# Attention with two gated layers on one core: later rounds for weight pieces and softmax reciprocals, marked copies, and two fill units in the scores' banks

## The chip, the cores and the metric

The kernel runs on one core of one Trainium2 chip, as a single launch. The metric is the time of one execution in device microseconds; smaller is better. The time before is a median of three runs. All times below are microseconds (us) unless marked ns.

## The reference

Three layers follow each other. Shapes: 2 batches, 12 heads, 448 positions, 64 columns a head; so the model width is 768, and the hidden width 1024.

```python
# 1. attention with a soft cap
scores = cap * tanh((q @ k.T) / sqrt(64) / cap)
attn   = exp(scores - max(scores))
attn   = attn / (sum(attn) + 1e-9)
x      = attn @ v                       # heads side by side: 2 x 448 x 768
# 2. gated layer with spatial mixing
h      = gelu_tanh(x @ w_in)            # 768 -> 1024
u, v   = halves of h                    # 512 each
v      = layernorm(v) * g_ln
v      = einsum('ts,bsd->btd', w_sg, v) + b_sg
x      = x + (u * v) @ w_out            # 512 -> 768
# 3. gated convolution
h      = relu(x @ w2_in)
c      = conv of 3 taps along positions
out    = (h * sigmoid(c)) @ w2_out
```

## The kernel before

**Attention.** Two heads make a pair; there are 12 pairs, N = 0 to 11. A pair is worked in two halves, so the loop `for R in range(2 * NN + LAGS[1])` has 26 rounds. In a round TensorE makes the scores of one half (`sc`, 4 PSUM banks, one buffer), and then, two rounds late, the products with the values and the sums of an earlier half (`pv`, 3 banks). ScalarE does two passes over each half: Tanh out of the bank (L387) and Exp in place (L388), so that the next scores can start once Tanh has read the banks. At the end of a pair ScalarE copies the products and the sums out of PSUM into `E` (L504); the next products wait for that copy.

**The softmax division.** For pairs 0 to 10 it is done off the path: GpSimd's queue moves the sums by DMA into a compact tile `ss` (L506), VectorE adds a guard and takes the reciprocal (L519, L520), DMAs spread it over the partitions as `rb` (L523, L529), and VectorE multiplies (L536); the result is split in a high and a low part, `X` (L105, L106). For the last pair, 11, there is no time for that: `norm_pe` copies the sums (L548), VectorE adds the guard and takes a reciprocal of 224 columns (L550, L551), and TensorE spreads it by multiplying with a selection matrix `sel` (L555).

**Pieces.** The weights come as 64-bit words and are converted on the chip. `w_in` comes in 12 pieces of 128x512, one per entry of `WIN`, which names the round of its load. A piece has three steps: s1 takes the top bits into a head tile `hd` (L149 on ScalarE, L151 on VectorE for the early ones), s2 joins them with the low bits (L154) and makes the high part (L160), s3 makes the low part (L163). There is one head tile, so a piece's s1 must wait for the s2 of the piece before it.

**What sets the order.** `later(k, fn)` puts a step k ticks ahead; a round has two ticks, one before and one after its value products. A scheduler then orders the instructions of each engine from this program. `pin(lasta)` and `pin(lastv)` keep a step behind the last marked instruction of ScalarE or VectorE. `ordered` keeps the attention's matmuls in the order written; matmuls of the later stages are not held by it. TensorE, ScalarE and VectorE each run their list in order, so that a waiting instruction holds all behind it.

**Fill units.** The first layer's units (`u_unit`, 18 matmuls each of 128x448) need the first weights and batch 0 only. Three of them are taken into attention as fill: `FILL` gives the round and which of the six steps. Each is summed in the single bank `mo` of pool `psm` and then goes through `gelu`: ScalarE L221, VectorE L224, ScalarE L225, VectorE L228. The next unit in that bank waits for L228. The fourth unit, here called unit 3 (L109 to L111), also uses the bank. After it come the units of the second half of `w_in` (`v_unit`, L724 to L726), and from there on matmuls alone.

**Names.** PE is TensorE, ACT ScalarE, DVE VectorE, POOL GpSimd, SP the queue of most loads. The lines that count: L149/L151, L154, L160, L163 (piece), L387, L388 (scores), L504 (copy of values), L519, L520 (sums), L536 (division), L548 to L559 (last pair), L221 to L228 (gelu).

Of the kernel before, what the change touches and what calls it, by code (L numbers as in the profile page):

```python
# [9 lines left out]
F32 = mybir.dt.float32  # L10
F32R = mybir.dt.float32r
U32 = mybir.dt.uint32
# [3 lines left out]
AF = mybir.ActivationFunctionType  # L16
# [3 lines left out]
P = 128  # L20
B, H, S, D = 2, 12, 448, 64
NPAIR = H // 2
DM, DF, DH = 768, 1024, 512
NK = DM // P
# [3 lines left out]
HS = S // 2  # L28
# [5 lines left out]

NFAST = 1

FILL = {14: (0, 0, 2), 18: (0, 2, 4), 22: (0, 4, 6), 23: (1, 0, 6), 25: (2, 0, 6)}

TAKEN = 3

# [1 line left out]

IDLE = 4

WIN = (3, 5, 8, 10, 12, 14, 15, 17, 18, 20, 21, 22)
WOS = (0, 1, 4, 7, 7, 10, 11, 15)
W2I = (12, 12, 13, 13, 15, 17, 22, 24, 26, 30, 30, 33)
W2O = (0, 0, 1, 3, 4, 6, 7, 8, 8, 10, 10, 11, 11, 11, 11, 12, 13, 14, 15, 17, 18, 18, 19, 19)
# [3 lines left out]
def stages(  # L52
# [17 lines left out]
    nc = tc.nc  # L70
    V, A, T, G = nc.vector, nc.scalar, nc.tensor, nc.gpsimd

    now = [0]
    lasta, lastv, lastr, lasts = [None], [None], [None], [None]

    def pin(last):
        return tc.issue_after(last[0].ins) if last[0] is not None else ExitStack()
# [11 lines left out]
    def later(k, fn):  # L89
        due.setdefault(now[0] + k, []).append(fn)  # L90
# [7 lines left out]
    def f(ap):  # L98
        return ap.bitcast(F32)
# [19 lines left out]
    psm = ctx.enter_context(tc.tile_pool(name="psm", bufs=1, space=PSUM))  # L119
# [12 lines left out]
    heads = []  # L132
# [35 lines left out]
    def decode(hi, lo, src, pool, bufs, wait=(1, 2, 3), hi_eng="a", cols=512, low_eng="v", top_eng="a"):  # L168

        if heads:  # L170
            return decode_half(hi, lo, src, pool, bufs, wait, hi_eng, top_eng)
        n = src.shape[1]
        r = pool.tile([P, cols, 2], U32, tag="f64", name="f64", bufs=bufs)[:, :n]
        sync(r, src)
        h, l = r[:, :, 1], r[:, :, 0]

        def s1():
            with pin(lasta), pin(lastv):
                A.activation(f(h), f(h), AF.Copy, scale=2.0**-112)  # L179
                if low_eng == "a":  # L180

                    A.activation(l, l, AF.Copy, scale=0.93 * 2.0**-29)  # L182
                else:
                    V.tensor_scalar(
                        out=l, in0=l, scalar1=29, scalar2=None, op0=ALU.logical_shift_right
                    )

        def s2():
            V.scalar_tensor_tensor(  # L189
                out=l, in0=h, scalar=3, in1=l, op0=ALU.logical_shift_left, op1=ALU.bitwise_or  # L190
            )
            V.scalar_tensor_tensor(  # L192
                out=l, in0=h, scalar=0x80000000, in1=l, op0=ALU.bitwise_and, op1=ALU.bitwise_or
            )
            if hi_eng == "a":
                A.activation(hi, f(l), AF.Copy)
            else:
                V.tensor_copy(hi, f(l))

        def s3():  # L200
            V.tensor_tensor(out=lo, in0=f(l), in1=f(hi), op=ALU.subtract)

        for k, fn in zip(wait, (s1, s2, s3)):
            later(k, fn)

    def wdec(dst, src, k, c0, c1, pool, bufs, **kw):
        c = slice(c0 % dst.shape[3], c0 % dst.shape[3] + c1 - c0)
        decode(dst[:, 0, k, c], dst[:, 1, k, c], src[k * P : (k + 1) * P, c0:c1], pool, bufs, **kw)

    def wi_piece(src, h, k):  # L210
        return WI[h], src, k, h * DH, (h + 1) * DH
# [34 lines left out]
    def constants(pool):  # L246
        V.tensor_scalar(
            out=capc, in0=capt, scalar1=CAP_MAX, scalar2=-CAP_MAX, op0=ALU.min, op1=ALU.max
        )
        V.reciprocal(out=rcap, in_=capc if bounded else capt)  # L250
        V.tensor_scalar(
            out=qscale, in0=rcap, scalar1=1.0 / math.sqrt(D), scalar2=None, op0=ALU.mult
        )

        V.tensor_scalar(out=ncap, in0=capc, scalar1=-1.0, scalar2=None, op0=ALU.mult)
        V.tensor_tensor(out=ncap, in0=ncap, in1=capc, op=ALU.min)
        A.activation(guard, ncap, AF.Exp)
        V.tensor_scalar(out=guard, in0=guard, scalar1=1e-9, scalar2=None, op0=ALU.mult)
        heads[:] = [pool.tile([P, 512], U32, name=f"hd{i}") for i in range(1)]
        for t in heads:  # L260
            G.memset(f(t), 0.0)
        eye = pool.tile([P, P], F32, name="eye")
        make_identity(nc, eye)
        G.memset(nhalf, -0.5)
        return eye

    def columns(pool):
        sync(gbc, g_ln.partition_broadcast(P))
        decode(cw[:, 0], cw[:, 1], conv_w, pool, 4 if bounded else 3)

    def attention(att, psa):
# [218 lines left out]
        def norm(N, both):  # L490
            b, p = divmod(N, NPAIR)
            if N >= B * NPAIR - NFAST:
                return norm_pe(N, both)

            j = N % 2
            last = N == B * NPAIR - NFAST - 1
            m = 1 if last else 2
            if j == 0:
                pairs[:] = (
                    att.tile([P, 2 * (S + HS)], F32, tag="E", name="E", bufs=3),  # L500
                    att.tile([P, 14], F32, tag="ss", name="ss", bufs=2)[:, : 7 * m],
                )
            e, ss = pairs
            A.activation(e[:, j * (S + HS) : (j + 1) * (S + HS)], both, AF.Copy)  # L504
            u = j * (2 * S + HS)
            G.dma_start(ss[j * P // m : (j + 1) * P // m], e[::32, u : u + HS])  # L506
            if j == 0 and not last:
                return

            rb = att.tile([P, 2, S], F32, tag="rb", name="rb", bufs=2)  # L510
            eb = e[:, HS : HS + m * S].rearrange("p (j c) -> p j c", j=m)
            rb = rb[:, :m]

            ds = []


            def s1():
                with pin(lastv):
                    V.tensor_scalar(out=ss, in0=ss, scalar1=guard, scalar2=None, op0=ALU.add)  # L519
                V.reciprocal(out=ss, in_=ss)  # L520
                ds.append(dr.tile([m, 2, 2, HS], F32, tag=f"d{m}", name="d"))
                d = ds[0]
                G.dma_start(d.rearrange("j h f (p c) -> (j h f p) c", c=7 * m), ss)  # L523

            def s1b():
                (d,) = ds
                for h in range(2):
                    for i in range(m):
                        G.dma_start(  # L529
                            rb[h * D : (h + 1) * D, i].rearrange("p (f c) -> p f c", f=2),  # L530
                            d[i, h].partition_broadcast(D),
                        )

            def s2():
                with pin(lastv):
                    V.tensor_tensor(out=eb, in0=eb, in1=rb, op=ALU.mult)  # L536
                with pin(lasta):
                    lastv[0] = split(eb, X[:, 0, p - j : p + 1, b], X[:, 1, p - j : p + 1, b], "a")

            later(4, s1)  # L540
            later(5, s1b)
            later(13, s2)

        def norm_pe(N, both):

# [17 lines left out]
        fill = {}  # L563
        done = 0
        for R in range(2 * NN + LAGS[1]):
            N, half = divmod(R, 2)
            if R == 1:
                columns(att)
            if R == 4:
                load_vlast(3, NN)  # L570
            for j, at in enumerate(WIN):
                if at == R:
                    top_eng = "v" if R < 11 else "a"
                    wdec(*wi_piece(w_in, j // NK, j % NK), att, 4, hi_eng="v", wait=(3, 4, 5), top_eng=top_eng)
            if R < 2 * NN:
                if half == 0 and N + 2 < NN:
                    load(N + 2)
                if half == 0 and N + 1 < NN:
                    load_v(N + 1)
                if R == 1:  # L580

                    start_values(0)
                    scores(N, half, {2: lambda: value(0, 0), 3: lambda: value(0, 1)})
                    values(0, 0, True)
                    done += 1
                else:
                    scores(N, half)
                if half == 0 and N + 1 < NN:
                    prep_q(N + 1)
                    prep_k(N + 1)  # L590
            if R in FILL:

                i, k0, k1 = FILL[R]
                if k0 == 0:
                    fill[i] = psm.tile([P, 512], F32, tag="mo", name="mo")[:, :S]
                for k in range(k0, k1):
                    mmw(fill[i], 0, i, k, ordered)
                if k1 == NK:
                    u_done(0, i, fill[i])
            tick()  # L600
            if R - done >= LAGS[R >= LAGS[2]]:
                values(*divmod(done, 2))
                done += 1
            tick()
# [414 lines left out]
```

## Time and profile before

| | us |
|---|---|
| median of 3 runs | 335.48 (333.1 to 338.03) |
| the profiled execution | 337.11 |
| its span, first to last instruction | 335.3 |
| TensorE busy | 318.5 (95%) |
| VectorE busy | 238.3 (71%) |
| ScalarE busy | 223.2 (67%) |
| GpSimd busy | 37.6 (11%) |
| mean granted TensorE clock | 0.985 |

The kernel is a relay: attention up to about 121 us, where four engines and the DMA queues work side by side, and then dense matrix products to the end. A share of the whole span says little here; the views have to be read by stage. In a timeline row the columns are start, length, engine, line and operation, out<-in, shape, count; "idle" in brackets is the time the engine stood still just before and what ended it. In a windows row they are the stretch, its length, busy time (and instructions) of PE, PE's weight load, DVE, ACT, POOL, then the granted TensorE clock (1.00 is 2.4 GHz, 0.50 is 1.2 GHz), the DMA share and GB/s.

### The profile page before, as it was taken

What the parts mean: (1) busy time and instruction counts of PE and PEld (TensorE: products, weight loads), DVE (VectorE), ACT (ScalarE), POOL (GpSimd) and SP (SyncE); (2) the same over time, 40 slices, a digit from 0 to 9 for tenths busy, and PEclk for the clock granted to TensorE, in tenths of its full rate; (3) what the DMA queues carried; (4) which work ended last, traced back from release to release, by engine and by line L of the source; (5) the groups of instructions that cost most, each with busy time, mean ns of one, the idle gap of its engine ahead of it and who ended that gap; (6) DMA issues with size and microseconds to landing.
All of it is one profiled execution on the core that took longest, in us unless ns stands there. A gap on an engine that the chain in (4) does not pass through costs nothing.

```text
span 335.3 us, 6265 instructions
## 1 busy us (share of the span) xinstructions
PE 318.5 (95%) x2380; PEld 262.8 (78%) x2380; DVE 238.3 (71%) x471; ACT 223.2 (67%) x357; POOL 37.6 (11%) x74
## 2 busy tenths in 40 slices
PE   7979999999788999999999999999999999999992
PEld 6445666656556778988899999999999999999991
DVE  4556586585965589996998789996975999980000
ACT  2887999999896257675765565555855988873010
POOL 4000130440304320221111000000000000000000
PEclk9978999999999999999999999999999999999998
DMA  5586595778422134212323490002392123012211
GB/s 141 150 193 187 154 259 171 199 216 189 133 75 76 38 123 108 69 38 78 121 71 125 124 343 20 0 2 63 71 334 100 31 65 94 0 59 112 82 55 35
DMA packets 22062, 37.73 MB, mean 113 GB/s; under 512 B 7320, under 2 KB 14376, under 8 KB 22024
## 3 DMA queue, kind: packets, MB, share of 16 engines
q1 hardware_dynamic: 20152, 34.41, 34.3%
q0 software_dynamic: 1632, 2.61, 3.1%
q8 instruction: 20, 0.33, 0.4%
q10 hardware_dynamic: 240, 0.23, 0.3%
q14 instruction: 18, 0.15, 0.2%
HBM read 34.40 MB, written 2.79 MB: 111 GB/s over the span
## 4 chain that ended last, share of the span: by engine, by line
PE 79%; ACT 10%; DMA 4%; SPq 2%; issue 2%; DVE 1%; ACTq 0%; DVEq 0%
PE mo L109 18%; PE mo L110 18%; PE mo L111 18%; PE pv L373 8%; PE sc L373 6%; ACT raw L387 4%; PE mo L724 3%; PE mo L726 3%; PE mo L725 3%; SPq L83 2%; ACT raw L388 2%; PE mo L373 2%; DMA qr<-in_qT_dram 1%; ACT hd L149 1%; DMA f<-in_conv_w_dram 1%
## 5 line engine op out<-in xcount | busy, mean ns | idle before, releaser
L109 PE MATMUL mo<-X,WI 128*128 128x448 f32 x126 | 46.0, 367 | 0.3 <-DVE u L228 0.3
L110 PE MATMUL mo<-X,WI 128*128 128x448 f32 x126 | 46.0, 366 | 0.0
L111 PE MATMUL mo<-X,WI 128*128 128x448 f32 x126 | 45.9, 365 | 0.0
L373 PE MATMUL pv<-raw,V 128*32 128x224 f32 x576 | 34.6, 370 | 3.5 <-ACT E L504 3.3
L388 ACT ACTIVATE raw<-raw 128x1792 f32<-128x1792 f32 (+3 forms) x26 | 36.7, 1413 | 0.8
L387 ACT ACTIVATE raw<-sc 128x1792 f32<-128x1792 f32 (+1 forms) x22 | 32.4, 1472 | 5.0 <-PE sc L373 4.9
L110 PE MATMUL mo<-HG,W 128*128 128x448 f32 x96 | 34.8, 365 | 0.0
L111 PE MATMUL mo<-HG,W 128*128 128x448 f32 x96 | 34.7, 365 | 0.0
L109 PE MATMUL mo<-HG,W 128*128 128x448 f32 x96 | 34.1, 365 | 0.0
L373 PE MATMUL sc<-Q,K 64*128 64x448 f32 x216 | 29.9, 399 | 3.8 <-ACT raw L387 3.3
L373 PEld LDWEIGHTS pv<-raw,V 128*32 128x32 f32 x576 | 19.1, 112 | 16.6 <-ACT E L504 6.0
L373 PEld LDWEIGHTS sc<-Q,K 64*128 64x128 f32 x216 | 19.1, 192 | 14.7 <-ACT raw L387 8.1
L179 ACT ACTIVATE f<-f 128x256 f32<-128x256 f32 (+2 forms) x44 | 22.8, 518 | 10.2 <-DMA f<-in_w_out_dram 6.2
L189 DVE SCALAR_TENSOR_TENSOR f<-f 128x256 uint32<-128x256 uint32 (+2 forms) x44 | 22.3, 515 | 8.2 <-ACT f L182 8.0
L109 PEld LDWEIGHTS mo<-X,WI 128*128 128x128 f32 x126 | 23.6, 188 | 2.8 <-DVE u L228 0.8
L110 PEld LDWEIGHTS mo<-X,WI 128*128 128x128 f32 x126 | 23.7, 188 | 2.0
L111 PEld LDWEIGHTS mo<-X,WI 128*128 128x128 f32 x126 | 23.6, 188 | 2.0
L904 ACT ACTIVATE o<-mo 128x448 f32<-128x448 f32 x12 | 6.3, 542 | 24.7 <-PE mo L111 20.8
L182 ACT ACTIVATE f<-f 128x256 uint32<-128x256 uint32 (+2 forms) x44 | 22.7, 515 | 0.0
L192 DVE SCALAR_TENSOR_TENSOR f<-f 128x256 uint32<-128x256 uint32 (+2 forms) x44 | 22.4, 515 | 0.1
L110 PEld LDWEIGHTS mo<-HG,W 128*128 128x128 f32 x96 | 18.0, 188 | 1.4
L109 PEld LDWEIGHTS mo<-HG,W 128*128 128x128 f32 x96 | 18.0, 188 | 1.4
(148 smaller groups left out, 685.8 us busy)
## 6 DMA issues: line engine op xcount, KB each, us to landing
f<-in_w_in_dram SPq DMA_DIRECT2D x12, 512.0 KB, 4.4
f<-in_w_out_dram SPq DMA_DIRECT2D x24, 256.0 KB, 4.5
f<-in_w_in_dram SPq DMA_DIRECT2D x12, 511.8 KB, 5.1
f<-in_w_out_dram SPq DMA_DIRECT2D x8, 384.0 KB, 3.1
qr<-in_qT_dram SPq DMA_DIRECT2D x24, 112.0 KB, 3.7
out_dram<-o SPq DMA_DIRECT2D x12, 224.0 KB, 1.9
rb<-d POOLq DMA_DIRECT2D x22, 112.0 KB, 4.0
V<-in_vL_dram SPq DMA_DIRECT2D x12, 192.0 KB, 3.3
```

The costliest lines, as they stand in the source:

```text
L109: matmul(ps, lhsT=whi, rhs=xhi, start=start, stop=False)
L110: matmul(ps, lhsT=whi, rhs=xlo, start=False, stop=False)
L111: matmul(ps, lhsT=wlo, rhs=xhi, start=False, stop=stop)
L179: A.activation(f(h), f(h), AF.Copy, scale=2.0**-112)
L182: A.activation(l, l, AF.Copy, scale=0.93 * 2.0**-29)
L189: V.scalar_tensor_tensor(out=l, in0=h, scalar=3, in1=l, op0=ALU.logical_shift_left, op1=ALU.bitwise_or)
L192: V.scalar_tensor_tensor(out=l, in0=h, scalar=0x80000000, in1=l, op0=ALU.bitwise_and, op1=ALU.bitwise_or)
L373: lastm[0] = T.matmul(*args, **kw)
L387: A.activation(x, ps, AF.Tanh, **sc)
L388: lasta[0] = A.activation(x, x, AF.Exp, scale=creg)
L724: T.matmul(ps, lhsT=xs(0, k), rhs=WI[1][:, 0, k], start=k == 0, stop=False)
L725: T.matmul(ps, lhsT=xs(0, k), rhs=WI[1][:, 1, k], start=False, stop=False)
```

## The change

It has seven parts: (1) the copy of values into `E` now marks `lasta`, so that a piece's s1 that comes later in the program cannot be put ahead of it; (2) two head tiles in place of one; (3) the identity matrix is made only in the fallback program that does not run here; (4) for pairs below 8, s1 and s1b of the sums come two ticks later and s2 one tick later; (5) the steps of a piece come one tick later, and the load rounds of `WIN` change; (6) fill unit 1 starts in round 24 in place of 23; (7) fill units 1 and 2 are summed in banks 1 and 2 of a new tile `fi` that takes the place of the scores' tile, in place of the bank `mo`.

```diff
-FILL = {14: (0, 0, 2), 18: (0, 2, 4), 22: (0, 4, 6), 23: (1, 0, 6), 25: (2, 0, 6)}
+FILL = {14: (0, 0, 2), 18: (0, 2, 4), 22: (0, 4, 6), 24: (1, 0, 6), 25: (2, 0, 6)}
-WIN = (3, 5, 8, 10, 12, 14, 15, 17, 18, 20, 21, 22)
+WIN = (3, 5, 7, 9, 12, 15, 17, 19, 21, 22, 23, 24)
-        heads[:] = [pool.tile([P, 512], U32, name=f"hd{i}") for i in range(1)]
+        heads[:] = [pool.tile([P, 512], U32, name=f"hd{i}") for i in range(2)]
         for t in heads:
             G.memset(f(t), 0.0)
-        eye = pool.tile([P, P], F32, name="eye")
-        make_identity(nc, eye)
         G.memset(nhalf, -0.5)
-        return eye
+        if not bounded:
+            eye = pool.tile([P, P], F32, name="eye")
+            make_identity(nc, eye)
+            return eye
...
-            A.activation(e[:, j * (S + HS) : (j + 1) * (S + HS)], both, AF.Copy)
+            lasta[0] = A.activation(e[:, j * (S + HS) : (j + 1) * (S + HS)], both, AF.Copy)
...
-            later(4, s1)
-            later(5, s1b)
-            later(13, s2)
+            k = 6 if N < 8 else 4
+            later(k, s1)
+            later(k + 1, s1b)
+            later(14 if N < 8 else 13, s2)
...
-                    wdec(..., wait=(3, 4, 5), top_eng=top_eng)
+                    wdec(..., wait=(4, 5, 6), top_eng=top_eng)
...
                 if k0 == 0:
-                    fill[i] = psm.tile([P, 512], F32, tag="mo", name="mo")[:, :S]
+                    if i == 1:
+                        fill[3] = psa.tile([P, 4, 512], F32, tag="sc", name="fi", bufs=1)
+                    fill[i] = fill[3][:, i, :S] if i else psm.tile([P, 512], F32, tag="mo", name="mo")[:, :S]
```

In the changed kernel lines from 265 on have moved by one to four, so L373 of before is L374 there, L555 is L557, and L724 is L728.

**TensorE, end of attention.** From fill unit 2 to the selection matmul (`E,sel`) and the first `v_unit`. Before:

```order
L373 MATMUL mo<-X,WI_76 128x448 x18
L373 MATMUL pv<-raw,vlast 64x224 x4
L373 MATMUL pv<-raw,V 32x224 x8
L373 MATMUL pv<-raw,ones_152 32x224 x4
...
L109 MATMUL mo<-X,WI_76 128x448
...
L111 MATMUL mo<-X,WI_76 128x448
L555 MATMUL pv<-E,sel 64x224 x4
L724 MATMUL mo<-WI_77,X 128x512
```

Changed:

```order
L374 MATMUL pv<-raw,V 32x224 x16
L374 MATMUL pv<-sm,ones_149 32x224 x4
...
L111 MATMUL mo<-X,WI_76 128x448
L374 MATMUL fi<-X,WI_76 128x448 x18
L374 MATMUL pv<-raw,vlast 64x224 x4
L374 MATMUL pv<-raw,V 32x224 x8
L374 MATMUL pv<-raw,ones_149 32x224 x4
...
L557 MATMUL pv<-E,sel 64x224 x4
L728 MATMUL mo<-WI_77,X 128x512
```

The 18 matmuls of unit 3 (L109 to L111) stood between the last sums and the selection; now all of them stand ahead of fill unit 2, and the selection follows the last sums directly.

**VectorE, end of attention.** From the gelu of fill unit 2 to the reciprocal of the last pair. Before:

```order
L224 SCALAR_TENSOR_TENSOR g_1416<-g_1416,mo 128x448
L228 SCALAR_TENSOR_TENSOR u<-g_1416,mo 128x448
L536 TENSOR_TENSOR E<-E,rb 128x896
L550 TENSOR_SCALAR E<-E,one 128x224
L551 RECIPROCAL E<-E 128x224
```

Changed:

```order
L224 SCALAR_TENSOR_TENSOR g_1403<-g_1403,fi 128x448
L228 SCALAR_TENSOR_TENSOR u<-g_1403,fi 128x448
L537 TENSOR_TENSOR E<-E,rb 128x896
L154 SCALAR_TENSOR_TENSOR f_1327<-f_1327,hd_141 128x512
L552 TENSOR_SCALAR E<-E,one 128x224
L160 CAST WI_77<-f_1327 128x512
L553 RECIPROCAL E<-E 128x224
```

Two steps of the last piece (L154, L160) now stand between the gelu and the reciprocal.

**ScalarE, rounds 19 to 21.** The two passes over the scores (1792 and 1344 columns), the head copies `hd` and the copy of values `E`. Before:

```order
L149 ACTIVATE hd_141<-f_992 128x512
L387 ACTIVATE raw<-sc 128x1344
L388 ACTIVATE raw<-raw 128x1344
L149 ACTIVATE hd_141<-f_1034 128x512
L504 ACTIVATE E<-pv 128x672
L387 ACTIVATE raw<-sc 128x1792
```

Changed:

```order
L389 ACTIVATE raw<-raw 128x1792
L388 ACTIVATE raw<-sc 128x1344
L389 ACTIVATE raw<-raw 128x1344
L149 ACTIVATE hd_142<-f_978 128x512
L505 ACTIVATE E<-pv 128x672
L388 ACTIVATE raw<-sc 128x1792
```

One head copy has left the stretch; the other still stands ahead of the copy of values, and it writes the other head tile. In all, 7 head copies of 512 columns stood on ScalarE ahead of the last Tanh of attention; now 4 do, and 4 stand behind it.

## Rows read from the trace of the kernel before

**Rows 1.** Windows by stage: end of middle attention, its tail, and the products.

```profile
57.50:99.40 41.90, 38.97 (x552) 25.62 (x541) 29.63 (x55) 39.40 (x37) 11.62 (x20) 1.00 0.60 164
99.40:121.25 21.85, 19.17 (x185) 14.41 (x183) 14.02 (x23) 9.91 (x14) 6.44 (x11) 1.00 0.29 91
121.25:329.00 207.75, 207.75 (x1008) 188.77 (x1006) 161.18 (x318) 128.31 (x269) 10.33 (x14) 1.00 0.27 87
```

**Rows 2.** Timeline of TensorE, 57 to 99 us: the rows with a wait.

```profile
69.98 1.76 PE L373 MATMUL pv<-raw,V 128*32 128x224 f32 x32 [0.55 <-ACT E L504]
...
76.05 1.49 PE L373 MATMUL sc<-Q,K 64*128 64x448 f32 x12 [0.54 <-ACT raw L387]
...
87.64 1.76 PE L373 MATMUL pv<-raw,V 128*32 128x224 f32 x32 [1.79 <-ACT E L504]
```

**Rows 3.** Timelines of VectorE (two rows) and ScalarE ahead of the longest wait.

```profile
84.15 0.23 DVE L519 TENSOR_SCALAR ss<-ss,one 128x14 f32<-128x14 f32 x1 [4.29 <-DMA ss<-E]
...
85.52 0.68 DVE L154 SCALAR_TENSOR_TENSOR f<-f,hd 128x512 uint32<-128x512 uint32 x1
...
86.23 0.78 ACT L149 ACTIVATE hd<-f 128x512 f16<-128x512 bf16 x1 [1.13 <-DMA V<-in_vL_dram]
```

**Rows 4.** Timeline of TensorE, 98 to 122 us.

```profile
98.80 0.61 PE L373 MATMUL sc<-qr,kl 64*64 64x224 f32 x8
100.77 3.94 PE L373 MATMUL mo<-X,WI 128*128 128x448 f32 x18 [1.36 <-DVE u L228]
...
113.84 0.61 PE L373 MATMUL pv<-raw,vlast 64*64 64x224 f32 x8
...
115.16 0.96 PE L373 MATMUL pv<-raw,ones 128*32 128x224 f32 x16
116.47 0.47 PE L109 MATMUL mo<-X,WI 128*128 128x448 f32 x1 [0.34 <-DVE u L228]
...
120.34 0.98 PE L555 MATMUL pv<-E,sel 128*64 128x224 f32 x8
121.25 0.50 PE L724 MATMUL mo<-WI,X 128*128 128x512 f32 x1
```

**Rows 5.** Timeline of VectorE, 108 to 119 us.

```profile
108.14 0.73 DVE L154 SCALAR_TENSOR_TENSOR f<-f,hd 128x512 uint32<-128x512 uint32 x1
108.90 0.45 DVE L160 CAST WI<-f 128x512 fp32r<-128x512 f32 x1
...
115.79 0.62 DVE L228 SCALAR_TENSOR_TENSOR u<-g,mo 128x448 f32<-128x448 f32 x1 [0.65 <-ACT g L225]
...
117.33 0.33 DVE L550 TENSOR_SCALAR E<-E,one 128x224 f32<-128x224 f32 x1
117.70 1.55 DVE L551 RECIPROCAL E<-E 128x224 f32<-128x224 f32 x1
```

**Rows 6.** Windows of 2 us: the granted clock is the third figure from the right.

```profile
20.00:22.00 2.00, 0.13 (x4) 0.00 (x0) 1.58 (x3) 2.00 (x3) 0.68 (x1) 0.90 0.90 253
22.00:24.00 2.00, 1.76 (x10) 1.59 (x12) 1.37 (x5) 1.50 (x2) 0.00 (x0) 0.50 1.17 232
...
28.00:30.00 2.00, 2.00 (x27) 1.00 (x22) 1.69 (x4) 0.28 (x1) 0.00 (x0) 0.89 0.82 257
...
86.00:88.00 2.00, 0.36 (x8) 0.33 (x12) 2.00 (x7) 1.77 (x3) 0.00 (x0) 1.00 0.57 180
```

**Rows 7.** Timeline of TensorE, 22 to 34 us: equal groups at either clock.

```profile
22.24 2.61 PE L373 MATMUL sc<-Q,K 64*128 64x448 f32 x12 [2.11 <-ACT raw L387]
24.77 3.23 PE L373 MATMUL pv<-raw,V 128*32 128x224 f32 x32
...
33.40 1.76 PE L373 MATMUL pv<-raw,V 128*32 128x224 f32 x32
```

**Rows 8.** Timeline of GpSimd: the identity's last step, and the first power.

```profile
3.12 0.30 POOL masks.py:199 TENSOR_SCALAR_AFFINE_SELECT eye<-eye 128x128 f32<-128x128 f32 x1
...
136.20 1.00 POOL L741 TENSOR_TENSOR mv<-mv,one 128x1 f32<-128x1 f32 x1 [6.78 <-DVE mv L738]
```

More of the change, by code (lines that the diff above doesn't have):

```diff
@@ L573, in attention @@
                     top_eng = "v" if R < 11 else "a"
-                    wdec(*wi_piece(w_in, j // NK, j % NK), att, 4, hi_eng="v", wait=(3, 4, 5), top_eng=top_eng)
+                    wdec(*wi_piece(w_in, j // NK, j % NK), att, 4, hi_eng="v", wait=(4, 5, 6), top_eng=top_eng)
             if R < 2 * NN:
```

## The prediction, made before the result was known

> **What bounds the kernel now.** The windows by stage come first [rows 1], because the change touches attention alone. From 121.25 us to the end TensorE is busy 207.75 of 207.75 us: nothing is to be had there, and whatever moves the start of that stretch moves the end by as much. In 57.5 to 99.4 us TensorE is busy 38.97 of 41.90 us, so 2.93 us are idle, and ScalarE is busy 39.40: the two are a close race. In the tail, 99.4 to 121.25 us, TensorE is busy 19.17 of 21.85 us, so 2.68 us are idle, while ScalarE does 9.91. Up to about 57 us the lists of TensorE and ScalarE stand as before. So the change can take away at most 2.93 + 2.68 = 5.6 us, and has to be judged by what it takes in their place.
>
> The timeline of TensorE says what the idle time is. In the middle three waits make nearly all of it: 0.55, 0.54 and 1.79 us, each ended by ScalarE [rows 2]. For the longest, look back along the two other engines [rows 3]. VectorE stood 4.29 us for the DMA of the sums before L519; so L154 of a piece ended only at 86.20; the next head copy started at 86.23, because it overwrites the one head tile that L154 reads (the row names a DMA, but the times fit L154); and the copy of values, which the products at 87.64 wait for, stood behind that head copy. In the tail [rows 4] fill unit 1 waits 1.36 us and unit 3 waits 0.34 us for L228, the end of the gelu that empties their common bank; the products between them wait 0.97 us for a copy of values, which is what is left of 2.68.
>
> **The change part by part.** The identity on GpSimd goes (its last step is the first row of [rows 8]) and a second head tile is cleared in its place, before GpSimd's first wait: nothing.
>
> *Head tiles, marked copies, later rounds of sums and pieces* work on one place and go together. L519 of pairs below 8 comes a round later, so VectorE is not held for the DMA; two head tiles part a head copy from the piece ahead; and ScalarE has three head copies fewer before its last Tanh. At 0.78 us each [rows 3] that is 2.3 us less, 37.1 us against TensorE's 38.97 in the same stretch: the race is decided for TensorE. Where a head copy still stands ahead of the copy of values, a wait can stay; I leave one of the shorter size, 0.55 us [rows 2]. Gain 2.93 - 0.55 = 2.4 us. Ends: 0 (all waits stay) and 2.93. The moved head copies land in the tail, where ScalarE has room; their VectorE steps come below. Loads move with `WIN`, still a round or more ahead of their use; SP's queue is in order, but the loads of scores pass the moved pieces forward, not back.
>
> *Fill units in the scores' banks.* TensorE now runs the products of pair 10, two matmuls of unit 3, fill 1, and so on. Fill 1 must wait for the last Tanh, which comes while the products run; unit 3 for the gelu of fill 0, which before ended 1.36 us after the scores [rows 4] and now has those products ahead of it; the products of pair 11 for a copy that is done some microseconds earlier. All 2.68 us of waits in the tail go.
>
> *What comes instead.* The selection matmul needs the reciprocal L551. Before, it had cover: the last sums were issued by 116.12, the 18 matmuls of unit 3 ran from 116.47 to 120.34, and L551 ended at 117.70 + 1.55 = 119.25 [rows 4, 5]. TensorE came 1.1 us after it. Now unit 3 is ahead of fill 2, and nothing stands between the last sums and the selection. Count from the end of fill 2, which is the start of the products at 113.84 [rows 4]. TensorE has 116.12 - 113.84 = 2.28 us of work. VectorE's chain through the gelu, the division and L550 took 119.25 - 113.84 = 5.41 us; now L154 (0.7 us) stands ahead of L550, and L160 (0.45 us, about half of it in the gap that L551 needs behind L550 anyway) ahead of L551 [rows 5]: 6.3 us. So TensorE waits 6.3 - 2.28 = **4.0 us**, with the whole list behind it: the `v_unit` matmuls are ready, but come later. Ends: 3.1 us (both steps hidden) and 4.7 (one more step of 0.7 us ahead of it). The tail becomes 21.85 - 2.68 + 4.0 = 23.2 us: **1.3 us longer**.
>
> *The clock.* A wait of TensorE has cost more than its length once: it had 0.13 us of work in 20 to 22 us, and the mean clock of 0.90 there says that it fell to 1.2 GHz at 21.6, some 1.5 us after the last matmul; by the mean of 0.89 in 28 to 30 us it came back at 28.4 [rows 6]. The same 32 matmuls took 3.23 us there and 1.76 us later [rows 7], so a microsecond at that level loses 0.46. The wait of 1.79 us at 86 us left it at 1.00 [rows 6]. A wait of 4.0 us is twice either; I take it that the clock falls. The low stretch lasted 6.8 us. If it starts 1.5 us into the wait, 2.5 us of it cost nothing and 4.3 us lose 2.0; if it starts near the end of the wait, as at 21.6 with 0.6 us left, 6.2 us lose 2.8. I take 2.4, the middle. Ends: 0 and 2.8.
>
> The Trainium skill says of this in "TensorE: Matmul & The Clock Gate", section Terms, that the penalty is about the throttled time times the share of pulses withheld. By that, as an estimate, the 6.8 us would cost 3.4 and the sum below would be 1.0 us higher, 337.8; the rows show 2.8, since part of the stretch had no matmul to slow, and the measurement decides.
>
> Sum: -2.4 + 1.3 + 2.4 = **+1.3 us**. The profiled execution took 337.1 us (a span of 335.3 and 1.8 around it) and becomes 338.4. It lay 1.6 us above the median of 335.5; the difference carries over: **336.8 us**.
>
> **The rivals.**
>
> *B: the clock holds.* The wait of 4.0 us comes, but no fall. For it: 1.79 us at 86 us without one, and dense matmuls ahead of the new wait, where the fall at 21.6 followed small ones. Against it: twice the length. Time: 335.5 - 2.4 + 1.3 = 334.4.
>
> *C: the middle is not cured.* The change would not do what its first part says: in the new list a head copy still stands ahead of four copies of values, so the waits on ScalarE stay. Against it: the three head copies fewer, and the freed head tile. Time: 335.5 + 1.3 + 2.4 = 339.2.
>
> *D: GpSimd's code, the slow side.* In the order the untimed instruction of GpSimd that stood ahead of the identity's last step, and that in the built program names a code library, now stands directly ahead of the first power of the layer norm. Its price is in no row; at 3.12 us it left no gap [rows 8], which bounds it by nothing there, if it was not running in the back. It decides beyond 6.8 us, the time that GpSimd stood idle before that power [rows 8]; then ScalarE's norm step, and the gelus queued behind it, are late. Banks for about two further units of some 4 us cover as much again, so it would have to take over 15 us; at 23 us the end moves by 8, on top of the forecast less the clock's 2.4: 342.4. Little speaks for it.
>
> **How the numbers follow.** Forecast 0.50, B 0.25, C 0.15, D 0.04; 0.06 for a mixture outside these. The time is the forecast's, 336.8. The forecast alone runs from 335.5 (all of the middle gained, the low stretch mostly idle) to 339. For 8 in 10 the range takes in B with the full middle and the short wait, 335.5 - 2.9 + 0.4 = 333.0, and most of C, with the longer wait and the full clock price 335.5 + 2.0 + 2.8 = 340.3; I cut that to 340. Two per cent of 335.5 is 6.7 us, about what a measurement of this kernel can tell from no change: 328.8 to 342.2. No case but D leaves it, and 5.6 us is all there is to gain: faster 0.02, within 0.93, slower 0.05.
>
> **What would show it.** Right: in the changed trace TensorE's idle time between 57 and the last scores is under 1 us; no wait for L228 in the tail; one wait of about 4 us before the selection, ended by VectorE's reciprocal; a mean clock near 0.5 in the 2 us windows behind it; TensorE without waits from there on. Wrong: the scores of pair 11 end at 99.4 or later (C); the clock is 1.00 in those windows (B); the selection starts within 2 us of the last sums, which would mean that the chain on VectorE is shorter than counted, and the time falls to 332 or below; a wait on GpSimd's power beyond 2 us (D).

## The result, and the profile after

The changed kernel takes 338.88 us (median of 13 executions, 336.73 to 340.06) against 335.89 for the kernel before beside it (13 executions, 333.1 to 338.03): ratio **1.0087, 95% interval 1.0061 to 1.0113**. That is 2.9 us slower, inside two per cent and inside the range on record; the forecast was 1.3 us slower. The profiled execution has a span of 337.1 us (335.3 before) and a mean granted clock of 0.983 (0.985).

The windows by stage of the changed kernel answer to [rows 1]; the first is of equal length with the 41.60 us that end 0.6 us behind the start of the last scores of before, where TensorE was also 2.93 us idle.

```profile
57.27:98.87 41.60, 40.31 (x566) 26.68 (x568) 27.21 (x50) 39.47 (x35) 10.97 (x19) 1.00 0.54 161
98.87:122.06 23.19, 19.10 (x184) 14.44 (x175) 16.64 (x29) 10.53 (x14) 6.87 (x12) 0.98 0.39 113
122.06:331.00 208.94, 208.94 (x1007) 189.63 (x1006) 162.25 (x319) 128.96 (x269) 10.23 (x14) 0.99 0.27 87
```

Idle time of TensorE in the middle is 1.29 us (the mark on record was under 1), in the tail 23.19 - 19.10 = 4.09, and none behind it. The timeline of TensorE, 57 to 124 us, has three waits of more than 0.25 us (the kernel before had six):

```profile
76.44 1.48 PE L374 MATMUL sc<-Q,K 64*128 64x448 f32 x12 [0.69 <-ACT raw L388]
...
86.78 1.76 PE L374 MATMUL pv<-raw,V 128*32 128x224 f32 x32 [0.55 <-ACT E L505]
...
98.27 0.61 PE L374 MATMUL sc<-qr,kl 64*64 64x224 f32 x8
...
110.58 3.83 PE L374 MATMUL fi<-X,WI 128*128 128x448 f32 x18
114.35 0.61 PE L374 MATMUL pv<-raw,vlast 64*64 64x224 f32 x8
...
115.67 0.96 PE L374 MATMUL pv<-raw,ones 128*32 128x224 f32 x16
120.72 1.41 PE L557 MATMUL pv<-E,sel 128*64 128x224 f32 x8 [4.09 <-DVE E L553]
122.06 0.80 PE L728 MATMUL mo<-WI,X 128*128 128x512 f32 x1
122.65 0.63 PE L729 MATMUL mo<-WI,X 128*128 128x512 f32 x1
```

The waits for L228 are gone, and the selection waits 4.09 us. VectorE's timeline ahead of it answers to [rows 5]:

```profile
116.30 0.62 DVE L228 SCALAR_TENSOR_TENSOR u<-g,fi 128x448 f32<-128x448 f32 x1 [0.64 <-ACT g L225]
116.84 1.08 DVE L537 TENSOR_TENSOR E<-E,rb 128x896 f32<-128x896 f32 x1
117.84 0.69 DVE L154 SCALAR_TENSOR_TENSOR f<-f,hd 128x512 uint32<-128x512 uint32 x1
118.44 0.33 DVE L552 TENSOR_SCALAR E<-E,one 128x224 f32<-128x224 f32 x1
118.69 0.42 DVE L160 CAST WI<-f 128x512 fp32r<-128x512 f32 x1
119.02 1.55 DVE L553 RECIPROCAL E<-E 128x224 f32<-128x224 f32 x1
```

From the end of fill 2 (114.35) to the end of the reciprocal it is 6.22 us. The clock, in windows of 2 us (third figure from the right):

```profile
118.00:120.00 2.00, 0.00 (x0) 0.00 (x0) 2.00 (x4) 0.90 (x1) 0.00 (x0) 1.00 0.92 262
120.00:122.00 2.00, 1.28 (x8) 0.69 (x8) 2.00 (x4) 0.00 (x0) 0.00 (x0) 0.78 0.71 254
122.00:124.00 2.00, 2.00 (x7) 1.56 (x6) 1.93 (x5) 1.31 (x3) 1.22 (x1) 0.50 0.00 0
124.00:126.00 2.00, 2.00 (x9) 1.64 (x8) 2.00 (x3) 1.71 (x5) 1.16 (x1) 0.87 0.00 0
```

A mean of 0.78 over 120 to 122 means 0.88 us at 1.2 GHz, so the clock fell at 121.1; with 2.0 and 0.52 us in the next two windows it was low for 3.4 us, all of it under work.

The middle holds something new. Timelines of VectorE, GpSimd and ScalarE ahead of the wait at 76.44, and VectorE's next division, changed kernel:

```profile
61.32 0.23 DVE L520 TENSOR_SCALAR ss<-ss,one 128x14 f32<-128x14 f32 x1
...
62.74 0.58 POOL L524 DMA_DIRECT2D d<-ss  x1 [6.96 <-DVE ss L521]
...
67.09 2.58 POOL L530 DMA_DIRECT2D rb<-d  x4 [3.15 <-PE sc L374]
...
73.13 1.09 DVE L537 TENSOR_TENSOR E<-E,rb 128x896 f32<-128x896 f32 x1 [2.77 <-DMA rb<-d]
...
74.26 0.95 ACT L105 ACTIVATE X<-E 128x896 fp32r<-128x896 f32 x1 [0.54 <-DVE E L537]
...
88.97 1.09 DVE L537 TENSOR_TENSOR E<-E,rb 128x896 f32<-128x896 f32 x1 [3.71 <-DMA rb<-d]
```

VectorE no longer waits for the sums ahead of L519 (4.29 us in [rows 3]); it now waits 2.77 us one step later, in the division, for the DMA that spreads the reciprocal. ScalarE's conversion of the result waits for that, the next Tanh stands behind the conversion, and the next scores wait 0.69 us for the Tanh. The same steps in the kernel before: the sums and the division of one pair of pairs (VectorE), then the DMAs of the next (GpSimd).

```profile
53.24 0.23 DVE L519 TENSOR_SCALAR ss<-ss,one 128x14 f32<-128x14 f32 x1 [3.93 <-DMA ss<-E]
...
68.94 0.57 POOL L523 DMA_DIRECT2D d<-ss  x1 [5.84 <-DVE ss L520]
...
70.60 1.08 DVE L536 TENSOR_TENSOR E<-E,rb 128x896 f32<-128x896 f32 x1
...
71.44 2.18 POOL L529 DMA_DIRECT2D rb<-d  x4 [1.93 <-DMA d<-ss]
```

### The profile page after: what moved, and what is told of

The parts are those of the page before. It is cut to its first block, busy times and chain, and to the rows that moved or that the text cites. A ratio compares the mean times of both kernels' runs of the same rounds, so it can differ in the third digit from the quotient of the medians.

```text
span 337.1 us, 6266 instructions
## 1 busy us (share of the span) xinstructions
PE 319.8 (95%) x2380; PEld 264.2 (78%) x2380; DVE 239.5 (71%) x471; ACT 223.4 (66%) x357; POOL 37.4 (11%) x73
## 3 DMA queue, kind: packets, MB, share of 16 engines
q0 software_dynamic: 1632, 2.61, 2.9%
HBM read 34.40 MB, written 2.79 MB: 110 GB/s over the span
## 4 chain that ended last, share of the span: by engine, by line
PE 84%; ACT 5%; DMA 4%; SPq 2%; DVE 2%; issue 1%; POOL 1%; ACTq 0%; DVEq 0%
PE mo L110 18%; PE mo L109 18%; PE mo L111 18%; PE pv L374 10%; PE sc L374 7%; PE mo L728 3%; PE mo L729 3%; PE mo L730 3%; ACT raw L388 2%; SPq L83 2%; PE fi L374 2%; PE mo L374 1%; DMA f<-in_conv_w_dram 1%; DMA qr<-in_qT_dram 1%; DMA rb<-d 1%; ACT raw L389 1%
## 5 line engine op out<-in xcount | busy, mean ns | idle before, releaser
L109 PE MATMUL mo<-X,WI 128*128 128x448 f32 x126 | 46.1, 367 | 0.0
L111 PE MATMUL mo<-X,WI 128*128 128x448 f32 x126 | 45.9, 365 | 0.0
L374 PE MATMUL pv<-raw,V 128*32 128x224 f32 x576 | 34.5, 370 | 0.8 <-ACT E L505 0.5
L111 PE MATMUL mo<-HG,W 128*128 128x448 f32 x96 | 34.7, 365 | 0.0
L374 PE MATMUL sc<-Q,K 64*128 64x448 f32 x216 | 29.8, 399 | 5.0 <-ACT raw L388 4.6
L109 PE MATMUL mo<-HG,W 128*128 128x448 f32 x96 | 34.1, 365 | 0.0
L374 PEld LDWEIGHTS sc<-Q,K 64*128 64x128 f32 x216 | 19.2, 192 | 15.6 <-ACT raw L388 9.9
L179 ACT ACTIVATE f<-f 128x256 f32<-128x256 f32 (+2 forms) x44 | 22.7, 517 | 10.8 <-DMA f<-in_w_in_dram 6.0
L374 PEld LDWEIGHTS pv<-raw,V 128*32 128x32 f32 x576 | 19.1, 112 | 13.6 <-issue 6.1
L109 PEld LDWEIGHTS mo<-X,WI 128*128 128x128 f32 x126 | 23.6, 188 | 2.4 <-issue 0.4
L111 PEld LDWEIGHTS mo<-X,WI 128*128 128x128 f32 x126 | 23.6, 188 | 2.0
L437 DVE TENSOR_TENSOR sm<-raw 128x896 f32<-128x896 f32 x12 | 13.1, 1089 | 15.4 <-ACT raw L389 15.4
L110 PEld LDWEIGHTS mo<-HG,W 128*128 128x128 f32 x96 | 18.0, 188 | 1.4
```

The source lines that it names most:

```text
L109: matmul(ps, lhsT=whi, rhs=xhi, start=start, stop=False)
L110: matmul(ps, lhsT=whi, rhs=xlo, start=False, stop=False)
L111: matmul(ps, lhsT=wlo, rhs=xhi, start=False, stop=stop)
L374: lastm[0] = T.matmul(*args, **kw)
L437: V.tensor_tensor(out=held[N], in0=raw[:, 0:2], in1=raw[:, 2:4], op=ALU.add)
```

## The experiments

Two measures serve in all of them. "Middle" is TensorE's idle time in 41.60 us that end 0.6 us behind the start of the last scores, from one profile. "Low" is the mean time at 1.2 GHz over the timed executions, worked out as twice (1 - mean granted clock) times the span, since the clock has two levels.

| kernel | ratio, 95% interval | middle | wait before the selection | low |
|---|---|---|---|---|
| the change | 1.0087 (1.0061 to 1.0113) | 1.29 | 4.09 | 11.3 |
| e1 parts 1 to 5 | 0.9994 (0.9959 to 1.0029) | 2.09 | none | 6.3 |
| e2 parts 6 and 7 | 1.0041 (0.9999 to 1.0083) | 1.68 | 2.46 | 9.9 |
| e3 unit 3 behind | 1.0033 (0.9990 to 1.0076) | 1.99 | 0.21 | 9.6 |
| e4 wait filled | 1.0017 (0.9979 to 1.0055) | 2.05 | filled | 6.5 |
| e5 unit 3 under the chain | 0.9997 (0.9962 to 1.0032) | 1.33 | 2.36 | 8.9 |
| e6 chain cleared too | 0.9949 (0.9918 to 0.9981) | 1.65 | none | 7.1 |
| e7 chain cleared alone | 1.0064 (1.0029 to 1.0100) | 1.71 | 3.02 | 10.1 |
| e8 = e1, old rounds | 1.0030 (1.0000 to 1.0059) | 2.60 | none | 8.5 |
| e9 = e1, old sums | 0.9959 (0.9922 to 0.9996) | 1.09 | none | 5.3 |
| e10 = e6, old sums | 0.9914 (0.9874 to 0.9954) | 0.73 | none | 7.2 |
| e11 = e6, sums half way | 0.9906 (0.9867 to 0.9944) | 0.65 | none | 7.1 |

The kernel before had 6.3, 6.8 and 6.6 us of low time beside the three groups (e1 to e4, e5 to e8, e9 to e11), over the executions that the ratios use, and 2.93 us of idle time in the middle.

"Middle" has to be read with care, because it differs between executions of one list of instructions. In this stretch e2 has the lists of the kernel before, and 1.68 us in place of 2.93. The change, e1 and e3 to e7 share their lists too, and have 1.29 to 2.09.

**e1 and e2: the change in two halves.** e1 keeps parts 1 to 5, e2 is the kernel before with parts 6 and 7 alone.

```diff
-FILL = {..., 24: (1, 0, 6), 25: (2, 0, 6)}
+FILL = {..., 23: (1, 0, 6), 25: (2, 0, 6)}
-                    fill[i] = fill[3][:, i, :S] if i else psm.tile([P, 512], F32, tag="mo", name="mo")[:, :S]
+                    fill[i] = psm.tile([P, 512], F32, tag="mo", name="mo")[:, :S]
```

> The change with parts 6 and 7 undone: fill units 1 and 2 again in rounds 23 and 25 and in the bank mo, all else as changed. Theory A (the loss is the lost cover: the selection waits about 4 us for the reciprocal because unit 3 no longer stands between, and the clock falls behind that wait): unit 3 covers the reciprocal again, the waits of the tail (2.7 us) come back, the middle keeps its gain of about 1.6 us; 334 to 335.5 us, ratio to before 0.995 to 0.999, no wait of the selection. Rival B (the loss comes from parts 1 to 5, the later rounds and head copies): as slow as the change, 338.9, ratio 1.009.

> Before with parts 6 and 7 alone: fill units 1 and 2 in the scores' banks, head tiles, copies, rounds as before. Here 3 matmuls of unit 3 stay behind the last sums and the steps of the last piece are not in VectorE's chain. Theory A: the three waits of the tail go (2.7 us) and a wait of the selection of about 2.7 us comes; the middle keeps its waits; 335.5 to 337.5 us, ratio 1.000 to 1.005, the upper end if the clock falls. Rival B: only gain, 333.2, ratio 0.992. Rival C (sums in the scores' banks are slow in themselves): 338.9 or more.

e1 gains nothing that can be measured: -0.2 us, interval -1.4 to +1.0, where the sum on record had -2.4 for the same parts; the ratio lies just above its expected range. So the loss is not made by these parts, but the gain is missing. Its profile shows the new wait larger than in that of the change, though the lists are the same there; VectorE, ScalarE, TensorE:

```profile
73.99 1.09 DVE L537 TENSOR_TENSOR E<-E,rb 128x896 f32<-128x896 f32 x1 [3.58 <-DMA rb<-d]
...
75.12 0.95 ACT L105 ACTIVATE X<-E 128x896 fp32r<-128x896 f32 x1 [1.34 <-DVE E L537]
...
77.30 0.87 PE L374 MATMUL sc<-Q,K 64*128 64x448 f32 x6 [1.50 <-ACT raw L388]
```

In e2 the selection waits and the clock falls (TensorE's timeline, then the windows):

```profile
118.79 1.64 PE L555 MATMUL pv<-E,sel 128*64 128x224 f32 x8 [2.46 <-DVE E L551]
...
118.00:120.00 2.00, 1.21 (x8) 0.82 (x8) 2.00 (x3) 0.00 (x0) 0.00 (x0) 0.74 0.93 348
```

Its middle shows something else: VectorE's L519 and the products, to be set beside [rows 3] and [rows 2].

```profile
82.60 0.23 DVE L519 TENSOR_SCALAR ss<-ss,one 128x14 f32<-128x14 f32 x1 [3.08 <-DMA ss<-E]
...
86.62 1.76 PE L373 MATMUL pv<-raw,V 128*32 128x224 f32 x32 [0.57 <-ACT E L504]
```

The longest wait of the middle, 1.79 us in the profile of before, is 0.57 here with the same lists: the sums' DMA, issued at 78.49 (78.27 before), let L519 begin at 82.60 in place of 84.15.

**e3: all 18 matmuls of unit 3 held behind the last sums.**

```diff
-                    mmw(ps, b, i, k)
+                    mmw(ps, b, i, k, behind if n == TAKEN else T.matmul)
```

`behind` is a matmul under `pin(lastm)`, behind the last ordered matmul of attention.

> The change with unit 3 held behind the last sums of attention, so that its 18 matmuls stand ahead of the selection as before; nothing else moved. Theory A: the wait of the selection falls from 4.1 to about 1.3 us, the clock holds; fill 2 now waits about 1.3 us for the gelu of fill 1, which unit 3 had covered; in all 1.5 us of waits and 1.6 us of clock less than the change: 334.5 to 336 us, ratio 0.995 to 1.000. Rivals B and C: 338.9, ratio 1.009.

The cover works, as TensorE's timeline shows, but a wait opens elsewhere: fills 1 and 2 are slices of one tile, so fill 2 waits for the gelu of fill 1 once unit 3 no longer stands between them.

```profile
107.00 5.49 PE L373 MATMUL fi<-X,WI 128*128 128x448 f32 x18 [2.41 <-DVE u L228]
...
118.78 0.98 PE L556 MATMUL pv<-E,sel 128*64 128x224 f32 x8 [0.21 <-DVE E L552]
```

The 18 matmuls took 5.49 us in place of 3.83: the clock fell here instead (0.77, 0.50, 0.87 in the windows from 106 to 112). So the ratio came out above its expected range, and it cannot price the cover; that took e5 and e6.

**e4: the wait filled.** The change, with 15 more matmuls ahead of the selection, whose result the selection overwrites.

```diff
+            for _ in range(15):
+                ordered(rp, lhsT=WI[0][:, 0, 0, :P], rhs=X[:, 0, 0, 0], start=True, stop=True)
```

> The change with 15 added matmuls of 128x448 ahead of the selection, whose products nobody reads: they fill the wait for the reciprocal with work, so that the clock has no reason to fall, while the selection starts at the same time. If the clock's fall costs what the rows show (about 1.6 us): 337.3 us, ratio 1.004, and no window under 1.00 behind the selection. If the fall costs nothing beside the wait: 338.9, ratio 1.009.

```profile
116.21 3.33 PE L374 MATMUL pv<-X,WI 128*128 128x448 f32 x15 [0.99 <-ACT E L550]
119.47 0.98 PE L559 MATMUL pv<-E,sel 128*64 128x224 f32 x8
...
120.00:122.00 2.00, 2.00 (x13) 1.41 (x10) 2.00 (x5) 0.73 (x2) 1.22 (x1) 1.00 0.02 8
```

TensorE's list is no shorter and the selection still comes when the reciprocal is done, yet the clock stays at 1.00 and the selection takes 0.98 us in place of 1.41. The ratio falls from 1.0087 to 1.0017, below the expected 1.004. That is about 2.3 us, between 0.8 and 3.9 by the intervals of the two comparisons. The low time falls by 4.8 us, from 11.3 to 6.5, of which the second fall makes 3.4 in the profile; the other 1.4 us lie, as far as the profiles show, in the early low stretch, and would make some 0.6 of the 2.3 us (an estimate, at the 0.46 that [rows 7] give). So the clock's fall makes the larger part of the loss, and the rest of the change is +0.6 us, interval -0.7 to +1.8.

**e5 and e6: unit 3 under the chain, then the chain cleared.** e5 puts only fill 2 into the scores' banks. Fill 1 and unit 3 share `mo`, so that unit 3 waits for fill 1's gelu and comes to stand behind the last sums. e6 also holds the first VectorE step of a piece and the division behind the last reciprocal (`lastd`).

```diff
-                    if i == 1:
+                    if i == 2:
...
-                    fill[i] = fill[3][:, i, :S] if i else psm.tile(...)
+                    fill[i] = fill[3][:, i, :S] if i == 2 else psm.tile(...)
# e6, besides:
-            V.reciprocal(out=r, in_=r)
+            lastd[0] = lastv[0] = V.reciprocal(out=r, in_=r)
...
+            with pin(lastd):
                 V.scalar_tensor_tensor(out=low, ...)        # L154
...
-                with pin(lastv):
+                with pin(lastv), pin(lastd):
                     V.tensor_tensor(out=eb, in0=eb, in1=rb, op=ALU.mult)
```

> The changed kernel with one line different: only fill unit 2 is summed in the scores' banks, fill unit 1 goes back to the bank mo. Unit 3, which also uses mo, then has to wait for the gelu of fill 1 and falls behind the last sums of its own accord, so that its 18 matmuls (3.7 us) lie under VectorE's chain again; and fill 2, in another tile, waits for no gelu (in the run with unit 3 pinned it waited 2.4 us). Theory A (the change is worth its idle time in the middle, less the lost cover of the selection, less the clock's fall behind that wait): no wait for L228; the wait before the selection is 6.3 - 2.3 - 3.7 = 0.3 us if VectorE's list stays as it is, up to 2.5 us if the steps of a piece get ahead of the gelu of fill 2 there (1.8 us of them); tail waits of 0.3 to 2.5 in place of 2.68, middle 1.6 us shorter: 335.3 less 1.8 to 4.0, so 331.3 to 333.5, ratio 0.988 to 0.995; with 2.5 us and a fall of the clock about 335.5, 1.001. Rival C (the scores' banks cost something in themselves, whatever stands ahead of the selection): half of it stays, so 1.004, as the banks alone gave.

> As the run before it, and also the first VectorE step of a piece and the division are held behind the last pair's reciprocal, so that the chain from the gelu of fill 2 to the selection has only the guard and the reciprocal in it. Theory A: chain of about 4.3 us from the end of fill 2, TensorE has 2.3 + 3.7 = 6.0 us of work there: no wait before the selection, none for a gelu in the tail, no second fall of the clock. The tail loses all of its 2.68 us, the middle its 1.6: 335.3 - 4.3 = 331.0, ratio 0.987. The steps held back (two pieces, 3.6 us of VectorE) are needed 2.7 us after the first v_unit begins; if that is too late, a wait of 1 to 2 us comes there and the ratio is 0.991. Rival C: 1.00 or above.

e5 came out above its range, near the 1.001 named for a fall of the clock. Its wait was 2.36 us, near the upper end: L520, L154, L160 and L163 (110.43 to 112.76) stood ahead of the gelu of fill 2. In the profile the clock held behind that wait, and the first `v_unit` came at 119.26, 2.0 us sooner than before; but its low time over all executions, 8.9 us, is 2.1 above that of the kernel before beside it, and two executions have 14 us where that kernel has at most 10.8; so the clock seems to fall in some of them. In e6 the selection follows unit 3 without a wait:

```profile
115.36 0.37 PE L111 MATMUL mo<-X,WI 128*128 128x448 f32 x1
115.65 0.98 PE L558 MATMUL pv<-E,sel 128*64 128x224 f32 x8
```

The selection starts 4.7 us sooner than in [rows 4] (3.1 us when counted from the last scores), but the ratio gives back part of it: from the first `v_unit` to the end of the span it is 215.3 us against 214.05 before. Of these 1.3 us TensorE's idle time between 116 and 220 makes 0.5; the rest is not located. The size was missed, the direction held, and rival C of the expectations (banks that cost something in themselves) falls: the same banks are in use here.

**e7: the chain cleared, unit 3 as in the change.**

> The changed kernel with its banks and its unit 3 ahead of fill 2 as they are, and only VectorE's list changed: the first step of a piece and the division are held behind the last pair's reciprocal. Theory A with the step as the prediction has it: what stood ahead of the guard and the reciprocal (division 0.9, L154 0.7, L160 half of 0.45) leaves the chain, so the wait of 4.09 us before the selection shrinks, but only until ScalarE's copy of the last pair bounds it: that ended at 117.57 in the changed kernel, so the reciprocal could end near 119.5 in place of 120.57, and the wait is 3.0 to 3.1 us. The clock's fall stays: ratio 1.006 against 1.009 of the changed kernel. If a wait of 3 us does not bring the clock down: 0.999. If the wait stays at 4 us, something else than these steps sets it.

```profile
115.13 0.70 ACT L551 ACTIVATE E<-pv 128x672 f32<-128x672 f32 x1
...
115.87 0.34 DVE L553 TENSOR_SCALAR E<-E,one 128x224 f32<-128x224 f32 x1 [0.66 <-ACT E L551]
116.24 1.55 DVE L554 RECIPROCAL E<-E 128x224 f32<-128x224 f32 x1
...
117.94 1.63 PE L558 MATMUL pv<-E,sel 128*64 128x224 f32 x8 [3.02 <-DVE E L554]
```

The wait is 3.02 us and ScalarE's copy now bounds it, as expected; the clock still falls (0.53 and 0.62 in the windows from 118 to 122). The two steps of the piece and the division were worth 1.07 us of the 4.09.

**e8 and e9: which part of the middle gains, which loses.** e8 is e1 with the old `WIN` and the old steps, e9 is e1 with part 4 undone.

```diff
# e8
-WIN = (3, 5, 7, 9, 12, 15, 17, 19, 21, 22, 23, 24)
+WIN = (3, 5, 8, 10, 12, 14, 15, 17, 18, 20, 21, 22)
-                    wdec(..., wait=(4, 5, 6), top_eng=top_eng)
+                    wdec(..., wait=(3, 4, 5), top_eng=top_eng)
# e9
-            k = 6 if N < 8 else 4
+            k = 4
-            later(14 if N < 8 else 13, s2)
+            later(13, s2)
```

> The kernel of the first experiment (parts 1 to 5 of the change, fill units as before) with part 5 undone: the old load rounds of the pieces and their steps one tick earlier; the second head tile, the marked copies and the later sums stay. Theory P (the rounds of the pieces, which take head copies away from ScalarE's stretch, make the middle's gain): TensorE's idle time in 57 to 99 us goes back from 1.3 to 2.3 us or more, and the ratio is about 1.003 higher than that experiment's 0.9994. Rival T (the second head tile and the later sums make it): idle stays at 1.3, ratio 0.999.

> The kernel of the first experiment (parts 1 to 5 alone) with part 4 undone: the sums' reciprocal, its DMA and the division at their old ticks, for all pairs. Theory W (the later reciprocal puts a wait in the place of the one it removes: in that experiment VectorE's division stood 3.58 and 1.44 us for the DMA that spreads the reciprocal, ScalarE's conversion behind it 1.34 us, and the scores at 77.30 waited 1.50 us): the division waits for no DMA; L520 again waits some 4 us for the sums; the scores at 76 to 77 us wait 0.7 us or less; idle time of TensorE in the middle 0.8 to 1.3 us in place of 2.1; ratio 0.9994 less 0.002 to 0.004. Theory V (the old wait returns with its old price): a wait of about 1.8 us before the products at 87, idle 2.5 to 2.9, ratio 1.001 to 1.003.

With the old rounds the middle is idle for 2.60 us and the ratio is 0.0036 higher, the values that theory P expected; its low time is also 1.7 us above that of the kernel before beside it, which may make a part of this (e1's is not). With the new rounds and the old sums the middle is idle for 1.09 us, and the ratio falls to 0.9959, with its interval below 1. Each of the two differences has an error of about 0.005, so the ratios alone prove neither. For the sums the traces speak too: the division waits for its DMA in all seven profiles of the change's list, here in none, and here and in e10 the middle is shorter (1.09 and 0.73 us) than in any of those. VectorE and ScalarE in e9:

```profile
66.64 0.24 DVE L520 TENSOR_SCALAR ss<-ss,one 128x14 f32<-128x14 f32 x1 [6.28 <-DMA ss<-E]
...
70.22 1.08 DVE L537 TENSOR_TENSOR E<-E,rb 128x896 f32<-128x896 f32 x1
...
71.36 0.93 ACT L105 ACTIVATE X<-E 128x896 fp32r<-128x896 f32 x1
```

The old wait for the sums is back, 6.28 us long, and costs TensorE little, it seems because nothing behind it is urgent any more; the wait in the division, though shorter, stands directly ahead of ScalarE's conversion and so of the Tanh.

**e10 and e11: the best version.** e6 with part 4 undone (e10, the edit of e9), and with the reciprocal one tick later than before in place of two (e11: `k = 5 if N < 8 else 4`).

> The kernel with the cleared chain (0.9949) with part 4 undone in the same way. Theory W: the scores near 75.7 wait 0.5 us or less in place of 1.04, and 0.5 to 1.0 us come off: ratio 0.992 to 0.994. Theory V: 1.3 us more, ratio 0.998 to 0.999.

> The kernel with the cleared chain, with the reciprocal of the sums one tick later than in the kernel before in place of two, and the division where the change has it. Theory W by sizes: the DMA that spreads the reciprocal is issued about half a round (some 3.5 to 4 us) earlier than in the changed kernel, which covers the 2.8 to 3.7 us that the division waited for it there, and VectorE's wait for the sums is below the 4 us of the old place: both waits near 0 to 1 us, scores near 75.7 without a wait beyond 0.3, ratio 0.991 to 0.994. If either wait stays at 3 us or more, 0.995 or above.

Both beat both kernels, the kernel before by 0.9%, which is inside two per cent; e10 is a little better than its expected range, e11 at the edge of its own. In e11 neither wait is left here, and 0.57 us for the next sums at 84.62 (VectorE, ScalarE; then the window of the middle):

```profile
69.28 0.23 DVE L521 TENSOR_SCALAR ss<-ss,one 128x14 f32<-128x14 f32 x1
69.41 1.08 DVE L538 TENSOR_TENSOR E<-E,rb 128x896 f32<-128x896 f32 x1
...
73.83 0.93 ACT L105 ACTIVATE X<-E 128x896 fp32r<-128x896 f32 x1
...
56.52:98.12 41.60, 40.95 (x582) 27.23 (x578) 26.79 (x48) 40.07 (x36) 11.85 (x21) 1.00 0.61 176
```

Its expectation named 3.5 to 4 us; in VectorE's list the one tick brought the guard ahead of the reciprocal 7.5 and 8.0 us forward (53.87 and 69.28, against 61.32 and 77.25 in the change). e10 and e11 cannot be told apart by time.

## Why the prediction was right in its kind and short in its size

- **The tail: right in its waits.** The chain was put at 6.3 us and is 6.22; the wait at 4.0 and is 4.09; all 2.68 us of old waits went. From the last scores to the first `v_unit` it was 22.45 us and is 23.79: 1.34 longer, forecast 1.3. But 0.43 of that is the selection at the low clock, which the next point counts; the tail alone is 0.9 longer, and the sum on record put 0.4 too much there. e6 and e7 show that the cover and the steps ahead of the reciprocal are its causes.
- **The clock: right that it falls, too dear, and wrong in its parts.** The fall was placed within the wait, with a stretch of 6.8 us, part of it idle. It came 0.4 us after TensorE had gone back to work, and lasted 3.4 us, all of it under work. In the profile that costs 1.55 us: 0.43 in the selection, 1.12 in the next six `v_unit` matmuls, which took 2.61 us in place of 1.49 at the full clock (0.34 for the first, 0.23 for each other). The Trainium skill says in "TensorE: Matmul & The Clock Gate", section Terms, that the penalty is about the throttled time times the share withheld; as an estimate that makes 1.7 us of the 3.4, close to the 1.55 of the rows. 2.4 us were set down; e4's 2.3 agrees with that only within its wide interval and with some early low time in it, so the match is luck. Rival B (the clock holds) falls.
- **The middle: the step that failed.** "L519 of pairs below 8 comes a round later, so VectorE is not held for the DMA" was true of L519 alone. The program moves the reciprocal by two ticks and its division by one; in VectorE's list the sums' step came 8.1 us later (53.24, now 61.32), which is nearly two rounds, and the division 2.5 (70.60, now 73.13). Between them lies a chain of DMAs: in the change GpSimd issued `d` at 62.74 and `rb` until 69.67, and the division began when it had landed. That is 11.8 us, where the program of before left 17.4. So the division is held in L519's place: 2.77, 3.71 and 2.79 us in the change, up to 3.87 in e8. The trace of before had the durations: from L519 at 68.14 to the end of the issues of `rb` at 73.62 it is 5.5 us, and `rb` landed 4.0 us after its issue (median), 9.5 us together, an estimate. I followed the DMA ahead of the moved step and not those that the step issues itself.
- **The middle's size.** The gain of 2.4 us was worked out from 2.93 us of idle time and a wait of 1.79 us in one execution. e2, with the same lists there, had 1.68 and 0.57, so part of that gain is not to be had in each execution. The 1.6 us by which the profiled execution lay above the median were carried over as if they had nothing to do with that wait, which is not shown. Measured, the parts for which 2.4 us were set down gave 0.2 (e1); without part 4 they give 1.4, interval 0.1 to 2.6 (e9). How the missing 2.2 us divide between the division's wait and the size is open: e9 gives back 1.2, with an error of about 1.7.
- **What was left over.** With -0.2 for the middle, 0.9 for the tail and 1.55 for the clock the sum is +2.3; measured are +2.9, interval 2.0 to 3.8. So two errors worked against each other: the middle gained 2.2 us less than set down, and tail and clock cost about 1.2 us less. The range held because it took in most of rival C (the middle not cured, 339.2), whose time is the nearest. But its reason, head copies ahead of the copies of values, is behind only the 0.55 us at 86.78, and its sign, the scores of pair 11 at 99.4 or later, did not show: they end at 98.9.
- **GpSimd (rival D):** no wait for its power appears in the changed trace.
- The profiled execution was already 0.9 us late at 32 us, because ScalarE waited 2.33 us for the load of `conv_w`, 1.11 in that of before; in e1 to e4 it waited 1.02 to 2.62 us, so a single profile says nothing of the change there.

## What to carry to other kernels

When a step is moved later, follow every transfer that it starts to the instruction that needs it: a wait removed at the step can come back at its consumer, where it may cost more although it is shorter. An idle time before a dependent matmul is covered by work that doesn't depend on it; before moving such work, look for what else has stood under it. And a wait that brings the clock down is to be charged with the slow work behind it: here 1.55 us by the rows, against 0.9 us by which the tail itself grew. Before a gain is sized from a wait, look for the same wait in a second execution: here one was 1.79 us in one profile and 0.57 in another of the same lists.

## What the runs showed of the hardware

- The clock's second fall came after TensorE's work had begun again, in all four kernels that show it: at 121.1 (work from 120.72), 118.96 in e2 (118.79), 107.1 in e3 (107.00), 118.1 in e7 (117.94). Each time it was low for 3.4 us. The waits ahead were 4.09, 2.46, 2.41 and 3.02 us; behind 2.36 us in e5's profile it held. The early fall of the kernel before, at 21.6, came while TensorE still waited.
- The low time differs between executions of one kernel, and the time with it: the 27 executions of the kernel before that the ratios of e9 to e11 use have 3.3 to 10.7 us of it, with a correlation of 0.95 between low time and span, and a slope of 0.63 us of span for a us of low time. That goes with most of their scatter of 4.8 us. The slope is above the 0.46 that the slow matmuls of [rows 7] lose, so the low clock alone does not make it.
- The time that a small DMA needs differs too: with the same lists the sums of one pair of pairs let VectorE go on 5.9 us after GpSimd began to issue their DMA in the kernel before (78.27 to 84.15), and 4.1 us after it in e2 (78.49 to 82.60).
